# Key sums of an attention block by wide products with ones, and a reordered head, in an attention and bilinear feed-forward kernel

## The chip, the cores and the metric

The kernel runs on one core of a Trainium2 chip. The metric is the device time of one execution in microseconds, the median of several runs. The engines named below are TensorE (PE, matrix products; PEld are its weight loads), VectorE (DVE), ScalarE (ACT), GpSimd (POOL) and SyncE (SP), whose queue issues the DMA transfers here.

## The reference

Two blocks follow each other. Attention has 8 batches, 12 heads, 448 positions and 64 features a head; q and k are normalized by their root mean square and scaled by gains. The result, 3584 tokens of 768 features, goes through a bilinear feed-forward block with 1536 inner features.

```
def rmsnorm(x, g):
    rms = np.sqrt(np.mean(x * x, axis=-1, keepdims=True) + 1e-06)
    return x / rms * g
q_n, k_n = (rmsnorm(q, g_q), rmsnorm(k, g_k))
scores = scale * np.matmul(q_n, k_n.transpose(0, 1, 3, 2))
scores = scores - np.max(scores, axis=-1, keepdims=True)
attn = np.exp(scores)
attn = attn / (np.sum(attn, axis=-1, keepdims=True) + 1e-09)
x = np.matmul(attn, v)            # then (B,H,S,D) -> (B*S, H*D)
out = (x @ w_a) * (x @ w_b) @ w_out
```

The attention inputs are float32. The three weight matrices are float64 and reach the kernel as pairs of 32-bit words.

## The kernel before, in words

**The work.** Attention goes by pairs of heads: 6 pairs a batch, 48 in all. The 448 positions are split into four chunks of 112 (NJ = 4). For pair p, `loads` brings k, q and v; `normalize` squares and reduces k and q (L289 or L291, L297), takes the mean (L306), raises it to the power -0.5 on GpSimd (L310) and scales q with it (L314); `transposes` turns both (L331) and copies them out of PSUM with the gain (L336, L341 or L343). `scores` makes, chunk by chunk of keys, the transposed scores of both heads (L357) and their exponentials (L363, with k's scale folded in), which land as ET, keys on partitions. `values` multiplies ET with v and sums over the chunks in PSUM (L376). `sums_over_keys` makes the softmax denominators, `put_out` copies the values into xT (L479) and multiplies them by the inverted sums (L484).

**Key sums.** The first 12 pairs (LEAD = 12) and the others do it in two ways. From pair 12 on, VectorE and GpSimd add the four chunks of ET (L388, L390), two products with a matrix of ones spread the sums over 64 partitions a head (L406, `spread`), and VectorE inverts 128 x 448 values in PSUM (L409, `invert`). For the lead pairs TensorE does it from ET itself: `by_query` uses a 112 x 112 piece of ET as the stationary operand and one column of ones as the moving one, 2 heads x 4 query groups x 4 chunks, 32 products that the trace shows as 64 records (L416); `invert_few` inverts 112 x 8 values (L422), `to_features` spreads them by 8 products (16 records) with the identity (L428).

**The weights.** 72 units of 128 x 384 numbers (`weights`, L213 to L255): 48 of w_a and w_b, four column groups of 12, then 24 of w_out. Each is loaded as raw word pairs and made into float32 by one pass on ScalarE (L241), four on VectorE (L242, L243, L245, L247), a scaling of the low word, and a final add on GpSimd (L255). The low word is scaled by VectorE for every third unit (L250) and by ScalarE and GpSimd for the others (L253, L254). Units of w_a and w_b are staged in the place of w_out, so a w_out unit can only be written after the staging unit that lay there is done; w_out itself is staged in a ring of two buffers ("stage").

**Feed-forward.** `ffn` works by blocks of 384 or 512 tokens: 24 groups of input products (L510) into two PSUM buffers, taken out by ScalarE (L519) and VectorE (L521) into hT, then the output products (L534), which read w_out. There is one hT, and two xT buffers, so block 2 of xT (pairs from 12 on) opens when block 0 has been read.

**The order.** `Plan` writes the order of every engine's instructions before the kernel runs. Each step is booked by `op(engine, us, key, ...)` with a cost, a key and the buffers it reads and writes. The planner lets each engine take the step that can start first; among those that can start within 0.05 us of each other (0.2 us on TensorE) the lowest key goes first, and steps of one `chain` follow each other. Pair p's steps have key p, a weight unit n has n/4 + 1, loads two less, feed-forward products 10000 and more: they fill what is left. On the chip each engine goes through its list in that order.

Of the kernel before, what the change touches and what calls it, by code (L numbers as in the profile page):

```python
# [25 lines left out]
class Plan:  # L26
# [95 lines left out]
def kernel(  # L122
# [36 lines left out]
    NP = B * HP  # L159
# [4 lines left out]
    const = ctx.enter_context(tc.tile_pool(name="const", bufs=1))  # L164
# [9 lines left out]
    def setup(wk):  # L174
        grow = wk.tile([1, 2, D], FP32, tag="sq", name="grow")
        make_identity(nc, ident)
        nc.gpsimd.memset(expo, -0.5)
        nc.gpsimd.memset(ones, 1.0)
        for n, g in enumerate((g_q, g_k)):
            for e in range(2):  # L180
                nc.sync.dma_start(gain[e * D:(e + 1) * D, n:n + 1], g.rearrange("(d o) -> d o", o=1))
            nc.sync.dma_start(grow[:, n], g.rearrange("(o d) -> o d", o=1))

        nc.vector.scalar_tensor_tensor(gain[:, 0:1], gain[:, 0:1], float(D) ** -0.5, gain[:, 1:2],
                                       ALU.mult, ALU.mult)
        nc.vector.tensor_tensor(grow[:, 0], grow[:, 0], grow[:, 1], ALU.mult)
        nc.vector.tensor_reduce(grow[:, 1, 0:1], grow[:, 0], AX, ALU.max, apply_absolute_value=True)
        nc.vector.tensor_scalar(small, grow[:, 1, 0:1], LIMIT * D ** -0.5, None, ALU.is_le)
# [18 lines left out]
    def fast_body(ld, wk, ps_s, ps_o, ps_mm):  # L207
        plan = Plan()
        op, slot = plan.op, plan.slot
        LEAD = 12  # L210


        def weights(n):  # L213

            src, dst, kc, c = units[n]  # L220
            key = n / 4 + 1.0
            w = dst[:, kc, c * WC:(c + 1) * WC]
            wb, hold = w.bitcast(U32), {}
# [13 lines left out]

            lof = lambda: hold["lo"].bitcast(FP32)
            hif = lambda: hold["hi"].bitcast(FP32)
            op("SP", 0.1, key - 2.0, load, writes=[st], kb=384)  # L240
            op("ACT", 0.55, key, lambda: nc.scalar.activation(w, hif(), AF.Abs), [st], [name])  # L241
            op("DVE", 0.4, key, lambda: nc.vector.tensor_scalar(w, w, BELOW, ABOVE, ALU.max, ALU.min), [], [name])  # L242
            op("DVE", 0.4, key, lambda: nc.vector.tensor_scalar(  # L243
                wb, wb, 3, 0x3FFFFFFF, ALU.logical_shift_left, ALU.bitwise_and), [], [name])
            op("DVE", 0.56, key, lambda: nc.vector.scalar_tensor_tensor(  # L245
                wb, hold["hi"], 0xC0000000, wb, ALU.bitwise_and, ALU.bitwise_or), [st], [name])
            op("DVE", 0.56, key, lambda: nc.vector.tensor_scalar(  # L247
                hold["hi"], wb, 0xFF800000, None, ALU.bitwise_and), [name], [st])
            if n % 3 == 0:
                op("DVE", 0.56, key, lambda: nc.vector.scalar_tensor_tensor(  # L250
                    lof(), hold["lo"], 2.0 ** -52, hif(), ALU.mult, ALU.mult), [], [st])
            else:
                op("ACT", 0.55, key, lambda: nc.scalar.activation(lof(), hold["lo"], AF.Copy, scale=2.0 ** -52), [], [st])  # L253
                op("POOL", 1.05, key, lambda: nc.gpsimd.tensor_tensor(lof(), lof(), hif(), ALU.mult), [], [st])  # L254
            op("POOL", 1.05, key, lambda: nc.gpsimd.tensor_tensor(w, w, lof(), ALU.add), [st], [name])  # L255


# [3 lines left out]
        def loads(p, nm):  # L261
# [4 lines left out]
            def emit():  # L266
# [5 lines left out]
                    x = ld.tile([SP, 2, NJ * D], FP32, tag=nm, name=nm + "_sb")  # L272
                    nc.sync.dma_start(x, src[b, h0:h0 + 2].rearrange("h (p j) d -> p h (j d)", j=NJ))
                xs[nm, p] = x
            op("SP", 0.15, p - 2.0, emit, writes=[names[nm, p]], kb=230)

        def normalize(p):

            ms = names["ms", p] = slot("ms", 3)
            for s, nm in enumerate("kq"):  # L280
                sq, x = slot("sq", 1), names[nm, p]

                def square(nm=nm):
# [12 lines left out]
                        rs[p] = wk.tile([SP, 2, 2 * NJ], FP32, tag="ms", name="ms", bufs=3)  # L296
                    nc.vector.tensor_reduce(rs[p][:, "qk".index(nm)], xs["sq", nm, p], AX, ALU.add)  # L297
                if p < LEAD:
                    op("ACT", 0.65, p, square, [x], [sq])
                else:  # L300
                    op("POOL", 1.05, p, square, [x], [sq])
                op("DVE", 0.69, p, reduce, [sq], [ms])

            def mean():
                msf = rs[p].rearrange("p s n -> p (s n)")
# [6 lines left out]
            def apply():  # L312
# [3 lines left out]
                    xs["q", p].rearrange("p h (j d) -> p h j d", d=D),  # L316
                    rs[p][:, 0].rearrange("p (h j) -> p h j ()", j=NJ).to_broadcast([SP, 2, NJ, D]),
                    ALU.mult)
            op("DVE", 0.18, p, mean, [], [ms])
            op("POOL", 2.95, p, root, [], [ms])  # L320
            op("DVE", 0.7, p, apply, [ms, names["q", p]], [slot("qn", 1)])

        def transposes(p):
            sc = slot("sc", 2)
# [17 lines left out]
                else:  # L342
                    nc.vector.tensor_scalar_mul(qkTs[p][:, 0], x, gain[:, 0:1])  # L343
            T = names["qkT", p]
            op("PE", 0.9, p, turn, [names["k", p], "qn#0"], [sc], mode="full")
            op("ACT", 0.55, p, take_k, [sc], [T])
            op("ACT" if p < LEAD else "DVE", 0.68, p, take_q, [sc], [T])

# [45 lines left out]
            else:  # L394
                op("POOL", 2.1, p, emit, [E], [names["sum", p]])

        def sums_over_keys(p, chains):

            su = names["su", p] = slot("su", 1)

            def spread():
                sus[p] = ps_o.tile([P, S], FP32, tag="su", name="su")
                for e in range(2):
                    nc.tensor.matmul(sus[p][e * D:(e + 1) * D, :], lhsT=ones, rhs=sums[p][0:SP, e], start=True, stop=True)  # L406

            def invert():
                nc.vector.reciprocal(sus[p], sus[p])  # L409

            def by_query():
                sus[p] = ps_o.tile([P, S], FP32, tag="su", name="su")
                for e in range(2):
                    for j in range(NJ):
                        for c in range(NJ):
                            nc.tensor.matmul(sus[p][0:SP, e * NJ + j:e * NJ + j + 1],  # L416
                                             lhsT=ETs[p, c][:, e, j * SP:(j + 1) * SP], rhs=ones[:, 0:1],
                                             start=(c == 0), stop=(c == NJ - 1))

            def invert_few():  # L420
                rs["inv", p] = wk.tile([SP, 2 * NJ], FP32, tag="inv", name="inv", bufs=2)
                nc.vector.reciprocal(rs["inv", p], sus[p][0:SP, 0:2 * NJ])  # L422

            def to_features():
                for e in range(2):
                    for j in range(NJ):
                        n = e * NJ + j
                        nc.tensor.matmul(sus[p][e * D:(e + 1) * D, j * SP:(j + 1) * SP],  # L428
                                         lhsT=rs["inv", p][:, n:n + 1].to_broadcast([SP, D]),
                                         rhs=ident[0:SP, 0:SP], start=True, stop=True)  # L430
# [131 lines left out]
            weights(n)  # L562
        for p in range(NP + 1):
            if p < NP:
                for nm in "kqv":
                    loads(p, nm)
                normalize(p)
                transposes(p)
            if p > 0:
                values(p - 1, 2, f"A{p}")  # L570
                values(p - 1, 3, f"A{p}")
                if p - 1 < LEAD:
                    sums_over_keys(p - 1, (f"A{p}", f"B{p}"))
            if p < NP:
                scores(p, 0, f"A{p}")
                scores(p, 1, f"A{p}")
            if p > 0:
                if p - 1 >= LEAD:
                    sums_over_keys(p - 1, (f"A{p}", f"B{p}"))
                put_out(p - 1)  # L580
            if p < NP:
                values(p, 0, f"B{p}")
# [10 lines left out]
                ffn(p // HP - 2)  # L593
        ffn(B - 1)
        with tc.manual_schedule():
            setup(wk)
            plan.run()
        return plan

# [113 lines left out]
```

## Time and profile before

| what | value |
|---|---|
| median of 3 runs | 1896.07 us (1894.4 to 1897.51) |
| profiled execution | 1896.1 us |
| its span, first to last instruction | 1894.2 us |
| mean granted TensorE clock | 0.965 |
| busy: PE, DVE, ACT, POOL | 1853.9, 577.0, 406.2, 488.6 us |
| moved by DMA | 73.55 MB, mean 39 GB/s |

A row of a group has the line, the engine, the operation, the tiles written and read, their shapes and the count, then the busy time in us, the mean of one in ns, and the engine's idle time just before, with what ended it. A row of the timeline has the start and the length in us first. The matmuls' ends are modelled, so two groups can overlap a little.

### The profile page before, as it was taken

Reading aid. Unit: us, or ns where it says so; the run is one execution under the profiler, and the core shown is the slowest. Engines: PE = TensorE matmul, PEld = TensorE weight load, DVE = VectorE, ACT = ScalarE, POOL = GpSimd, SP = SyncE. Lnnn points to the kernel's source line nnn. Section 1 sums busy time; section 2 is a strip of 40 time slices with the busy share of each in tenths; the row PEclk is TensorE's granted clock in tenths of the full one; section 3 lists DMA queues with packets and bytes.
Section 4 is the critical chain, followed back from the end, with each engine's and each line's share of the span. In section 5 each row is a group of like instructions: output and inputs, shape, how many; then the busy total and the mean of one; then the engine's idle time right before and its main releaser. Section 6 shows DMA issues by size and latency. Waiting matters only on the chain.

```text
span 1894.2 us, 16866 instructions
## 1 busy us (share of the span) xinstructions
PE 1853.9 (98%) x6672; PEld 972.7 (51%) x6672; DVE 577.0 (30%) x824; ACT 406.2 (21%) x785; POOL 488.6 (26%) x324
## 2 busy tenths in 40 slices
PE   6799999999999999999999999999999999999998
PEld 3566665544444445544444445554444545554454
DVE  6788445344201441034201442034201430000000
ACT  5455334123201221023200231023201220000000
POOL 4566335234300441034300441034300410000000
PEclk9677889999999999999999999999999999999999
DMA  7451222111000210011100210011100100000000
GB/s 234 135 144 52 71 80 78 44 42 47 25 0 1 60 46 15 0 42 42 30 0 0 56 48 19 1 42 42 30 0 0 42 18 5 1 25 0 0 9 27
DMA packets 87325, 73.55 MB, mean 39 GB/s; under 512 B 49348, under 2 KB 78020, under 8 KB 87236
## 3 DMA queue, kind: packets, MB, share of 16 engines
q1 hardware_dynamic: 87236, 72.38, 13.4%
q8 instruction: 54, 0.88, 0.2%
q14 instruction: 35, 0.29, 0.0%
HBM read 61.34 MB, written 11.01 MB: 38 GB/s over the span
## 4 chain that ended last, share of the span: by engine, by line
PE 97%; DVE 1%; SPq 0%; ACT 0%; POOL 0%; DMA 0%; issue 0%; POOLq 0%; DVEq 0%; ACTq 0%
PE pf L510 46%; PE po L534 23%; PE sc L357 9%; PE o L376 8%; PE su L416 5%; PE pt L331 2%; PE su L406 2%; PE su L428 1%; ACT ET L363 0%; DMA w_out_sb<-in_moe_w_a_dram 0%; POOL sum L390 0%; POOL ms L310 0%; DVE su L409 0%; DVE w_a_sb L245 0%; DVE w_out_sb L247 0%
## 5 line engine op out<-in xcount | busy, mean ns | idle before, releaser
L510 PE MATMUL pf<-xT,w_b_sb 128*128 128x512 f32 (+1 forms) x1152 | 453.7, 542 | 0.0
L510 PE MATMUL pf<-xT,w_a_sb 128*128 128x512 f32 (+1 forms) x1152 | 453.1, 541 | 0.0
L534 PE MATMUL po<-w_out_sb,hT 128*128 128x384 f32 x1344 | 453.1, 490 | 0.0
L534 PEld LDWEIGHTS po<-w_out_sb,hT 128*128 128x128 f32 x1344 | 249.1, 190 | 192.5 <-issue 35.9
L510 PEld LDWEIGHTS pf<-xT,w_b_sb 128*128 128x128 f32 x1152 | 218.4, 191 | 219.4 <-issue 147.2
L510 PEld LDWEIGHTS pf<-xT,w_a_sb 128*128 128x128 f32 x1152 | 216.9, 190 | 217.8 <-issue 144.6
L363 ACT ACTIVATE ET<-sc,ms 112x448 f32<-112x448 f32 x384 | 213.6, 635 | 319.8 <-PE sc L357 317.6
L521 DVE TENSOR_TENSOR hT<-hT,pf 128x384 f32<-128x384 f32 (+1 forms) x96 | 59.6, 621 | 716.7 <-PE pf L510 716.7
L390 POOL TENSOR_TENSOR sum<-sum,ET 112x896 f32<-112x896 f32 x72 | 152.6, 2119 | 442.7 <-DVE sum L388 303.2
L519 ACT COPY hT<-pf 128x384 f32<-128x384 f32 (+1 forms) x96 | 51.1, 533 | 689.4 <-PE pf L510 689.4
L357 PE MATMUL sc<-qkT 64*112 64x448 f32 x768 | 189.0, 615 | 1.2 <-ACT qkT L341 1.2
L376 PE MATMUL o<-ET,v_sb 112*64 112x448 f32 x768 | 171.9, 556 | 0.0
L310 POOL TENSOR_TENSOR ms<-ms,expo 112x16 f32<-112x16 f32 x48 | 141.0, 2938 | 83.0 <-DVE ms L306 82.8
L409 DVE RECIPROCAL su<-su 128x448 f32<-128x448 f32 x36 | 106.8, 2967 | 122.2 <-PE su L406 122.2
L357 PEld LDWEIGHTS sc<-qkT 64*112 64x112 f32 x768 | 66.6, 188 | 103.9 <-issue 93.8
L416 PEld LDWEIGHTS su<-ones,ET 112*112 112x112 f32 x768 | 103.7, 229 | 9.1 <-PE o L376 3.5
L297 DVE TENSOR_REDUCE ms<-sq 112x8 f32<-112x512 f32 x96 | 65.4, 681 | 132.2 <-POOL sq L291 121.7
L416 PE MATMUL su<-ones,ET 112*112 112x1 f32 x768 | 104.7, 273 | 0.0
L376 PEld LDWEIGHTS o<-ET,v_sb 112*64 112x64 f32 x768 | 55.0, 140 | 87.6 <-issue 83.5
L314 DVE TENSOR_TENSOR qn<-q_sb,ms 112x512 f32<-112x512 f32 x48 | 62.9, 1310 | 85.0 <-issue 65.3
L462 POOL COPY xT<-tail 128x384 f32<-128x384 f32 x4 | 2.1, 520 | 311.9 <-PE pf L510 311.9
L543 DVE COPY o_sb<-po 128x384 f32<-128x384 f32 x28 | 15.6, 558 | 143.9 <-PE po L534 143.9
(60 smaller groups left out, 821.1 us busy)
## 6 DMA issues: line engine op xcount, KB each, us to landing
k_sb<-in_k_dram SPq DMA_DIRECT2D x96, 112.0 KB, 2.8
q_sb<-in_q_dram SPq DMA_DIRECT2D x48, 224.0 KB, 2.8
v_sb<-in_v_dram SPq DMA_DIRECT2D x48, 224.0 KB, 2.6
w_out_sb<-in_moe_w_a_dram SPq DMA_DIRECT2D x24, 384.0 KB, 3.9
w_out_sb<-in_moe_w_b_dram SPq DMA_DIRECT2D x24, 384.0 KB, 4.1
raw<-in_moe_w_out_dram SPq DMA_DIRECT2D x24, 384.0 KB, 3.1
out_dram<-o_sb SPq DMA_DIRECT2D x16, 168.0 KB, 2.1
out_dram<-o_sb SPq DMA_DIRECT2D x16, 144.0 KB, 2.0
```

The costliest lines, as they stand in the source:

```text
L297: nc.vector.tensor_reduce(rs[p][:, "qk".index(nm)], xs["sq", nm, p], AX, ALU.add)
L310: nc.gpsimd.tensor_tensor(msf, msf, expo, ALU.pow)
L314: nc.vector.tensor_tensor(qns[p].rearrange("p j h d -> p h j d"), xs["q", p].rearrange("p h (j d) -> p h j d", d=D), rs[p][:, 0].rearrange ...
L357: nc.tensor.matmul(t[:, e, 0:S], lhsT=qkTs[p][rows, 1, c * SP:(c + 1) * SP], rhs=qkTs[p][rows, 0, :], start=True, stop=True)
L363: nc.scalar.activation(E[:, e], scs[p, c][:, e, 0:S], AF.Exp, scale=rs[p][:, 1, 2 * c + e:2 * c + e + 1])
L376: nc.tensor.matmul(os_[p][e * D:(e + 1) * D, :], lhsT=xs["v", p][:, e, c * D:(c + 1) * D], rhs=ETs[p, c][:, e], start=(c == 0), stop=(c == ...
L390: nc.gpsimd.tensor_tensor(sums[p][0:SP], sums[p][0:SP], ETs[p, c], ALU.add)
L409: nc.vector.reciprocal(sus[p], sus[p])
L416: nc.tensor.matmul(sus[p][0:SP, e * NJ + j:e * NJ + j + 1], lhsT=ETs[p, c][:, e, j * SP:(j + 1) * SP], rhs=ones[:, 0:1], start=(c == 0), s ...
L510: nc.tensor.matmul(pfs[m, n][:, 0:N], lhsT=w_sb[:, c, m * P:(m + 1) * P], rhs=xTs[b][:, c, 0:N], start=(c == 0), stop=(c == KA - 1))
L521: nc.vector.tensor_tensor(x, x, y, ALU.mult)
L534: nc.tensor.matmul(held["po"][:, 0:HALF], lhsT=hTs[0][:, m, t * P:(t + 1) * P], rhs=w_out_sb[:, m, h * HALF:(h + 1) * HALF], start=(m == 0 ...
```

## The change

Five things change.

1. For the 12 lead pairs the key sums are made by `spread` too, fed by the four chunks of ET instead of their sum: 4 chunks x 2 heads products with the matrix of ones, summed in PSUM, then `invert` on VectorE. `by_query`, `invert_few` and `to_features` go.
2. The low word of every unit is scaled on VectorE.
3. Normalization (squares, reductions, mean, root, scaling of q) gets key p - 1.5 instead of p, and squares q before k.
4. The units of w_out get keys 11 to 12.9 instead of 13 to 18.75.
5. At the start, the loads of the gains go behind the q, k and v of pair 0, their use becomes a planned step, the test on the gains gets key 20, q is loaded ahead of k, an exponential of 128 zeros is computed first on ScalarE, and the planner books more time for loads on SP.

```
-            key = n / 4 + 1.0
+            key = n / 4 + 1.0 if n < 48 else 11.0 + (n - 48) / 12
...
-            op("SP", 0.1, key - 2.0, load, writes=[st], kb=384)
+            op("SP", 0.4, key - 2.0, load, writes=[st], kb=384)
...
-            if n % 3 == 0:
-                op("DVE", 0.56, key, lambda: nc.vector.scalar_tensor_tensor(
-                    lof(), hold["lo"], 2.0 ** -52, hif(), ALU.mult, ALU.mult), [], [st])
-            else:
-                op("ACT", 0.55, key, lambda: nc.scalar.activation(lof(), hold["lo"], AF.Copy, scale=2.0 ** -52), [], [st])
-                op("POOL", 1.05, key, lambda: nc.gpsimd.tensor_tensor(lof(), lof(), hif(), ALU.mult), [], [st])
+            op("DVE", 0.6, key, lambda: nc.vector.scalar_tensor_tensor(
+                lof(), hold["lo"], 2.0 ** -52, hif(), ALU.mult, ALU.mult), [], [st])
...
-            op("SP", 0.15, p - 2.0, emit, writes=[names[nm, p]], kb=230)
+            op("SP", 0.5 if nm != "k" else 1.0, p - (1.8 if nm == "v" else 2.0), emit, writes=[names[nm, p]], kb=230)
...
-            for s, nm in enumerate("kq"):
+            for s, nm in enumerate("qk"):
...
-                    op("ACT", 0.65, p, square, [x], [sq])
+                    op("ACT", 0.65, p - 1.5, square, [x], [sq])
...
-            op("DVE", 0.18, p, mean, [], [ms])
-            op("POOL", 2.95, p, root, [], [ms])
-            op("DVE", 0.7, p, apply, [ms, names["q", p]], [slot("qn", 1)])
+            op("DVE", 0.18, p - 1.5, mean, [], [ms])
+            op("POOL", 2.95, p - 1.5, root, [], [ms])
+            op("DVE", 0.7, p - 1.5, apply, [ms, names["q", p]], [slot("qn", 1)])
...
-            op("PE", 0.9, p, turn, [names["k", p], "qn#0"], [sc], mode="full")
+            op("PE", 0.9, p, turn, [names["k", p], "qn#0", "gain"], [sc], mode="full")
...
-                for e in range(2):
-                    nc.tensor.matmul(sus[p][e * D:(e + 1) * D, :], lhsT=ones, rhs=sums[p][0:SP, e], start=True, stop=True)
+                xss = [ETs[p, c] for c in range(NJ)] if p < LEAD else [sums[p][0:SP]]
+                for n, x in enumerate(xss):
+                    for e in range(2):
+                        nc.tensor.matmul(sus[p][e * D:(e + 1) * D, :], lhsT=ones, rhs=x[:, e],
+                                         start=(n == 0), stop=(n == len(xss) - 1))
...
-            if p < LEAD:
-                inv = slot("inv", 2)
-                op("PE", 3.2, p, by_query, [names["ET", p, c] for c in range(NJ)], [su], mode="full", chain=chains[0])
-                op("DVE", 0.2, p - 1, invert_few, [su], [inv])
-                op("PE", 0.9, p, to_features, [inv], [su], mode="cols", chain=chains[1])
-            else:
-                op("PE", 0.76, p, spread, [names["sum", p]], [su], mode="cols", chain=chains[1])
-                op("DVE", 3.0, p, invert, [], [su])
+            op("PE", 3.0 if p < LEAD else 0.76, p, spread,
+               [names["ET", p, c] for c in range(NJ)] if p < LEAD else [names["sum", p]],
+               [su], mode="cols", chain=chain)
+            op("DVE", 3.0, p, invert, [], [su])
...
+            if p == 0:
+                op("SP", 3.0, -1.9, load_gains, [], ["gain"], kb=1)
+                op("DVE", 0.2, -1.0, use_gains, [], ["gain"])
+                op("DVE", 0.6, 20.0, judge_gains, ["gain"], [])
...
-                    sums_over_keys(p - 1, (f"A{p}", f"B{p}"))
+                    sums_over_keys(p - 1, f"A{p}")
```

In the chains, a lead pair's sums now stand whole in chain A of the next pair, behind the last two values products and ahead of the first two scores; before, `by_query` stood there and `to_features` at the head of chain B.

More of the change, by code (lines that the diff above doesn't have):

```diff
@@ L172, with setup @@
     w_out_sb = const.tile([P, KO, DM], FP32, name="w_out_sb")
-    def setup(wk):
-        grow = wk.tile([1, 2, D], FP32, tag="sq", name="grow")
+    grow = const.tile([1, 2, D], FP32, name="grow")
+    def setup():
+        nc.scalar.activation(grow, nc.const_aps.tensor(0.0, [1, 2, D], FP32), AF.Exp)
         make_identity(nc, ident)
@@ L178, in setup, with load_gains @@
         nc.gpsimd.memset(ones, 1.0)
+    def load_gains():
         for n, g in enumerate((g_q, g_k)):
@@ L182, in setup, with use_gains, judge_gains @@
             nc.sync.dma_start(grow[:, n], g.rearrange("(o d) -> o d", o=1))
+    def use_gains():
         nc.vector.scalar_tensor_tensor(gain[:, 0:1], gain[:, 0:1], float(D) ** -0.5, gain[:, 1:2],
                                        ALU.mult, ALU.mult)
+    def judge_gains():
         nc.vector.tensor_tensor(grow[:, 0], grow[:, 0], grow[:, 1], ALU.mult)
@@ L298, in normalize @@
                 if p < LEAD:
-                    op("ACT", 0.65, p, square, [x], [sq])
+                    op("ACT", 0.65, p - 1.5, square, [x], [sq])
                 else:
-                    op("POOL", 1.05, p, square, [x], [sq])
-                op("DVE", 0.69, p, reduce, [sq], [ms])
+                    op("POOL", 1.05, p - 1.5, square, [x], [sq])
+                op("DVE", 0.69, p - 1.5, reduce, [sq], [ms])
             def mean():
@@ L395, in add_up, with sums_over_keys @@
                 op("POOL", 2.1, p, emit, [E], [names["sum", p]])
-        def sums_over_keys(p, chains):
+        def sums_over_keys(p, chain):
             su = names["su", p] = slot("su", 1)
@@ L408, in invert @@
             def invert():
                 nc.vector.reciprocal(sus[p], sus[p])
[L411 to L430, printed above, removed]
@@ L564, in fast_body @@
             if p < NP:
-                for nm in "kqv":
+                for nm in "qkv":
                     loads(p, nm)
+            if p == 0:
+                op("SP", 3.0, -1.9, load_gains, [], ["gain"], kb=1)
+                op("DVE", 0.2, -1.0, use_gains, [], ["gain"])
+                op("DVE", 0.6, 20.0, judge_gains, ["gain"], [])
+            if p < NP:
                 normalize(p)
@@ L578, in fast_body @@
                 if p - 1 >= LEAD:
-                    sums_over_keys(p - 1, (f"A{p}", f"B{p}"))
+                    sums_over_keys(p - 1, f"B{p}")
                 put_out(p - 1)
@@ L595, in fast_body @@
         with tc.manual_schedule():
-            setup(wk)
+            setup()
             plan.run()
```

## The prediction

> **What bounds the kernel now.** I read the page first, then the busy times by stretch, the chain of work that ended last, and the groups of instructions of the head.
>
> ```profile
> PE 1853.9 (98%) x6672; PEld 972.7 (51%) x6672; DVE 577.0 (30%) x824; ACT 406.2 (21%) x785; POOL 488.6 (26%) x324
> DVE  6788445344201441034201442034201430000000
> ```
>
> TensorE is occupied for 98% of the span and VectorE for 30%, but the second line shows that VectorE's work sits at the start: 6 to 8 tenths in the first four slices, nought to five later. The change touches the twelve lead pairs and the weight preparation, so only the head counts. I cut the span where the chain shows the sixth pair put out and feed-forward work starting (165.38), and where the last lead pair is through (325.48).
>
> ```profile
> 0.00:165.38 165.38, 132.65 (x746) 92.00 (x746) 126.47 (x235) 84.21 (x170) 91.30 (x85) 0.75 0.53 157
> 165.38:325.48 160.10, 160.10 (x874) 103.31 (x873) 79.49 (x149) 61.50 (x118) 70.70 (x55) 0.85 0.24 67
> 325.48:1894.20 1568.72, 1561.10 (x5056) 777.35 (x5056) 371.08 (x442) 260.54 (x498) 326.59 (x185) 1.00 0.08 23
> ```
>
> The columns are the stretch, its length, then busy time of PE, weight loads, VectorE, ScalarE and GpSimd, the granted clock, and the DMA share. From 325.48 on TensorE runs at clock 1.00 and stops only at the end: those 1568.7 us I keep as they are. The head is different. TensorE idles 165.4 - 132.7 = 32.7 us in the first stretch and none in the second, yet its granted clock is 0.75 and 0.85. One pair of the second stretch, from the chain (start, length, what), shows why:
>
> ```profile
> 173.58 8.79 PE su L416 x64
> 182.37 3.26 PE sc L357 x8
> 185.63 3.02 PE pf L510 x6
> 188.65 1.06 PE su L428 x13
> ...
> 191.50 1.69 PE sc L357 x8
> 193.19 2.13 PE pf L510 x6
> 195.33 0.77 PE pt L331 x8
> 196.10 1.95 PE pf L510 x6
> 198.05 1.65 PE o L376 x8
> ```
>
> The 64 narrow products of the key sums (L416, one moving column each) hold TensorE for 8.79 us, where the planner books 3.2. What follows pays too: eight score products take 3.26 us, and 1.69 a little later; six feed-forward products 3.02, and 1.95 to 2.13 later. So the narrow form costs its own time and a halved clock behind it.
>
> **The change part by part.** The sum is made against the profiled execution: span 1894.2, whole time 1896.1, so 1.9 us lie around the span; the median of the runs shown is 1896.07, the same.
>
> ```profile
> L416 PE MATMUL su<-ones,ET 112*112 112x1 f32 x768 | 104.7, 273 | 0.0
> L357 PE MATMUL sc<-qkT 64*112 64x448 f32 x216 | 67.5, 760 | 1.2 <-ACT qkT L341 1.2
> L376 PE MATMUL o<-ET,v_sb 112*64 112x448 f32 x208 | 53.0, 585 | 0.0
> L510 PE MATMUL pf<-xT,w_b_sb 128*128 128x384 f32 x60 | 23.8, 536 | 0.0
> L510 PE MATMUL pf<-xT,w_a_sb 128*128 128x384 f32 x61 | 22.6, 504 | 0.0
> L428 PE MATMUL su<-ident,inv 112*64 112x112 f32 x192 | 22.5, 320 | 0.0
> L331 PE MATMUL pt<-ident,qn 112*128 112x112 f32 x56 | 8.6, 280 | 20.1 <-DVE qn L314 20.1
> ```
>
> These are TensorE's groups from 0 to 325.48 (busy us, mean ns, idle before). *Removed:* L416 and L428, 104.7 + 22.5 = 127.2 us. *Added:* per lead pair four chunks for two heads, 16 records, with the shape of the values product L376 (112 rows, 64 stationary columns, 448 moving). Eight of those took 1.65 us, so 3.30 us a pair and 39.6 for twelve. They stand behind values in the same tile mode, so no switch is added.
>
> *Head work at full clock after the change.* A lead pair needs 2 x 1.65 (values) + 2 x 1.69 (scores) + 0.77 (transposes) + 3.30 = 10.75 us; twelve need 129.0. The head also holds 27 groups of eight score products, 26 of values and 14 pairs of transposes, that is 3, 2 and 2 beyond the lead: 5.1 + 3.3 + 1.5 = 9.9. It holds 121 feed-forward records, 20 groups of six at 2.04 (mean of 2.13 and 1.95): 40.8. Sum 179.7. Of the present 325.5, the same work without the wide sums is 140.1, removed products 127.2, idle 32.7; the remaining 25.5 is slow clock. So the span after is 1568.7 + 179.7 + L = 1748.4 + L, where L is what TensorE loses in the head by idling or a slow clock, and L is decided by VectorE, which gets all that the other engines give up.
>
> ```profile
> L245 DVE SCALAR_TENSOR_TENSOR w_a_sb<-w_out_sb,w_a_sb 128x384 uint32<-128x384 uint32 x11 | 11.7, 1064 | 0.4
> L243 DVE TENSOR_SCALAR w_a_sb<-w_a_sb 128x384 uint32<-128x384 uint32 x12 | 9.8, 818 | 0.3
> L245 DVE SCALAR_TENSOR_TENSOR w_b_sb<-w_out_sb,w_b_sb 128x384 uint32<-128x384 uint32 x11 | 8.9, 811 | 0.4
> L243 DVE TENSOR_SCALAR w_b_sb<-w_b_sb 128x384 uint32<-128x384 uint32 x11 | 8.3, 757 | 0.3
> L297 DVE TENSOR_REDUCE ms<-sq 112x8 f32<-112x512 f32 x8 | 5.3, 666 | 0.0
> L242 DVE TENSOR_SCALAR w_a_sb<-w_a_sb 128x384 f32<-128x384 f32 x12 | 4.6, 382 | 0.0
> L250 DVE SCALAR_TENSOR_TENSOR w_out_sb<-w_out_sb 128x384 f32<-128x384 uint32 x8 | 4.5, 557 | 0.2
> L247 DVE TENSOR_SCALAR w_out_sb<-w_a_sb 128x384 uint32<-128x384 uint32 x11 | 4.0, 361 | 0.4
> ...
> L314 DVE TENSOR_TENSOR qn<-q_sb,ms 112x512 f32<-112x512 f32 x3 | 3.4, 1121 | 0.0
> L484 DVE TENSOR_TENSOR xT<-xT,su 128x384 f32<-128x384 f32 x4 | 2.2, 554 | 7.7 <-PE su L428 7.7
> ```
>
> These are VectorE's groups from 80 to 160. A unit costs 0.38 (L242) + 0.79 (L243, both matrices) + 0.94 (L245) + 0.36 (L247), and 0.56 more where VectorE scales the low word (L250): 3.0 us. L243 and L247 do passes of one kind and size, 0.79 against 0.36; L245 and L250 likewise, 0.94 against 0.56. The excess of 0.81 a unit is waiting:
>
> ```profile
> 127.94 1.07 POOL L255 TENSOR_TENSOR w_a_sb<-w_a_sb,w_out_sb 128x384 f32<-128x384 f32 x1 [1.48 <-DVE w_out_sb L250]
> 128.17 1.06 DVE L243 TENSOR_SCALAR w_b_sb<-w_b_sb 128x384 uint32<-128x384 uint32 x1
> ```
>
> While GpSimd's add runs to 129.01, a pass of 0.36 takes 1.06 and ends behind it. Per three units GpSimd now has five such passes (three L255, two L254); after the change it has three. I scale the excess, 0.81 x 3/5 = 0.49, and take 2.7 us a unit. The bounds are 2.2 (no excess) and 3.0 (all of it). The Trainium skill (SBUF — State Buffer, Who interferes with whom) says that a VectorE pass in its two-port mode, or with two SBUF inputs, and a GpSimd pass exclude each other for the whole instruction. The trace agrees (1.06 for 0.36). By that rule the moved pass can now be held up in every unit, since it has two SBUF inputs; at one such loss of 0.70 a unit it would be 2.9, and the sum 11 us later.
>
> The second new burden is the reciprocal in PSUM, known from the later pairs:
>
> ```profile
> L409 DVE RECIPROCAL su<-su 128x448 f32<-128x448 f32 x36 | 106.8, 2967 | 122.2 <-PE su L406 122.2
> ```
>
> A lead pair then costs VectorE two reductions 1.33, mean 0.18 (as the planner books it), scaling of q 0.9 (between 0.69 booked and 1.12), division 0.65, reciprocal 2.97: 6.0 us. GpSimd and ScalarE, 91 and 84 busy of the first 165 us, lose work and bound nothing.
>
> *The order.* Normalization of a pair now has key p - 1.5, ahead of the weight units it used to stand behind. This goes:
>
> ```profile
> 59.29 1.01 PE L331 MATMUL pt<-ident,qn 112*128 112x112 f32 x4 [13.08 <-DVE qn L314]
> ```
>
> TensorE's 13.1 us of waiting for the third pair's q is a matter of order, not of capacity. What is late next is VectorE as a whole. The gain loads leave the front of the SP queue:
>
> ```profile
> 4.17 1.32 SPq L270 DMA_DIRECT2D k_sb<-in_k_dram  x2
> 10.23 0.69 DVE L297 TENSOR_REDUCE ms<-sq 112x8 f32<-112x512 f32 x1 [4.03 <-ACT sq L289]
> ```
>
> Six small loads stand ahead of the first k at 4.17. Moved behind pair 0's loads, they let the first reduction start near 7 instead of 10.2. The use of the gains becomes a wait in VectorE's queue with pair 0's and the first units' passes behind it, and the first transposes wait for it: 0 to 2 us, taken at nought, since pair 0's normalization runs beside the landing.
>
> *VectorE's account.* Up to the sixth pair's division it owes 17 units with key up to 5 (46 us), six pairs (36), the next normalization (2.4): from 7 to 91 without a wait, about 105 if a seventh of that time is waiting (now it idles 24% of the first stretch, behind TensorE). TensorE has 6 x 10.75 = 65 us of work until then: 40 lost. Up to the last unit of the third matrix it owes 72 x 2.7 = 194, 12 x 6.0 = 72, twelve hT products 7, two more pairs in part 6: from 7 to 286, with 8% of waiting 309 (a third of the present 24%, since it is now the scarce engine). TensorE's work that needs no third matrix is 129 + 9.9 + all 48 groups of the first block's input products (98), the rest of a pair and two begun output products (10): 247. So L = 309 - 247 = 62, and without waits 40, set by the first part.
>
> Sum: -127.2 + 39.6 - 25.5 + (62 - 32.7) = -83.8. Span 1810, time **1812**.
>
> **The rivals.**
>
> *VectorE keeps up.* The excess nearly vanishes and waits are few; L is then 30 to 40: 1780 to 1790, say 1786. For it: the 24% that VectorE idles now is time in which TensorE was the slow one. Against it: 48 more passes and 12 reciprocals, about 62 us, on an engine busy 126 of 165.
>
> *The third matrix comes late.*
>
> ```profile
> L255 POOL TENSOR_TENSOR w_out_sb<-w_out_sb,raw x24: 1004/1011/1472, 195.2 to 360.1; 128x384 f32<-128x384 f32 x24
> ```
>
> Its 24 units go through a ring of two buffers, load, ScalarE, VectorE, GpSimd, each load waiting for the add two units before. Now they take (360.1 - 195.2)/23 = 7.2 us each, but nothing hurries them: in the chain the first output product follows 54 us of input products. After the change they can start near 205 (unit 36 done). At 4.5 us they end at 309, as VectorE's account has it; at 5.8 at 338, L = 91 and the time is 1841.
>
> *The same, slower than before.* The ring decides alone from 147 us of L on, an end at 394, which is 8.2 us a unit. At 9 us: end 412, L = 165, time 1915. It needs a worse pace than the unhurried 7.2, with loads that stall in the SP queue behind q, k and v.
>
> *The clock stays low.* TensorE will idle over a third of the first 105 us. After the 13 us gap above, four transposes took 1.01 us, where eight take 0.77. If all of the first six pairs ran at half clock they would need 129 us, end near 137, and 32 us are added: 1844. Against it: pairs overlap, so most gaps are short. The Trainium skill (TensorE: Matmul & The Clock Gate, What's actually happening) has the clock fall to half after one idle window of about 3.4 us. The trace shows this behind gaps, but also behind L416 with no gap at all (3.26 against 1.69), so narrow products seem to count as idling.
>
> *The change doesn't deliver,* since the written order hangs together by something else: near 1896.
>
> ```profile
> 325.48 54.38 PE pf L510 x168
> 379.85 3.87 PE po L534 x12
> ```
>
> Against it: nothing but TensorE's own work stands in the second stretch, and these two rows show that the first output products had waited for input products alone.
>
> **How the numbers follow.** My forecast has 0.55 (1812); VectorE keeping up 0.16 (1786); third matrix late 0.18 (1841); clock low 0.06 (1844); slower 0.03 (1915); no change 0.02. The range of 1782 to 1846 covers units at 2.3 to 3.0 us and third-matrix ends from 280 to 341; it leaves out the low end of the second case and the last two. About 0.2% is what a measurement of this kernel tells from no change (three runs spread over 3.1 us). Faster 0.95, same 0.02, slower 0.03.
>
> **What would show it.** Right: sums of 16 wide products of 3.3 us; scores behind them at 1.69; granted clock above 0.9 in the second stretch; 48 reciprocals; VectorE over 85% busy to about 300; first output product between 290 and 330. Wrong: VectorE with long idle while TensorE waits (order), the first output product after 340 (ring), or a loss beyond the head.

## The result and the profile after

The changed kernel takes 1820.18 us (median of four runs, 1819.57 to 1821.77) against 1895.63 for the kernel before (1894.4 to 1897.51): a ratio of 0.960, 95% interval 0.9586 to 0.9619. The profiled execution spans 1817.8 us at a mean granted clock of 0.991. Of the experiments further down, one execution of run 2 took 4860 us beside three of about 1887, and the ratio of run 2 is that of the three.

First the page of the changed kernel: busy times, then the slices of VectorE and of the granted clock.

```profile
PE 1761.7 (97%) x5904; PEld 860.4 (47%) x5904; DVE 640.5 (35%) x872; ACT 384.3 (21%) x738; POOL 457.3 (25%) x276
...
DVE  7999998640023410443004420245002420000000
...
PEclk8999999999999999999999999999999999999999
```

TensorE has lost 92 us of busy time and 768 instructions. VectorE is now in its highest tenth for five slices of 45 us, and TensorE's clock is low in the first slice alone. The same by stretch (length, then busy time of PE, weight loads, VectorE, ScalarE, GpSimd, then clock, DMA share, GB/s):

```profile
0.00:120.00 120.00, 86.30 (x369) 33.12 (x370) 104.26 (x178) 67.78 (x134) 52.41 (x41) 0.90 0.58 174
120.00:200.00 80.00, 79.92 (x350) 35.50 (x351) 77.20 (x118) 40.68 (x79) 37.66 (x26) 1.00 0.37 102
200.00:340.00 140.00, 124.26 (x450) 62.58 (x450) 123.55 (x196) 38.40 (x77) 74.23 (x50) 0.98 0.31 87
340.00:1817.80 1477.80, 1471.23 (x4740) 729.22 (x4736) 335.45 (x383) 237.49 (x451) 292.98 (x160) 1.00 0.08 22
```

TensorE idles 33.7 us up to 120 and 15.7 us between 200 and 340, 49.5 in the head; before it idled 32.7, all in the first stretch. What it does there, and what it waits for (busy us, mean ns, idle before; up to 340 us):

```profile
L362 PE MATMUL sc<-qkT 64*112 64x448 f32 x250 | 58.3, 586 | 4.9 <-DVE qkT L348 3.6 <-ACT qkT L346 1.3
L491 PE MATMUL pf<-xT,w_b_sb 128*128 128x384 f32 x144 | 52.2, 508 | 9.8 <-DVE hT L502 9.8
...
L411 PE MATMUL su<-ET,ones 112*64 112x448 f32 x192 | 39.9, 559 | 0.0
L515 PE MATMUL po<-w_out_sb,hT 128*128 128x384 f32 x48 | 16.4, 492 | 0.0
L336 PE MATMUL pt<-ident,qn 112*128 112x112 f32 x64 | 10.1, 287 | 15.2 <-DVE qn L319 15.2
L336 PE MATMUL pt<-ident,k_sb 112*128 112x112 f32 x64 | 10.0, 282 | 13.7 <-ACT ET L368 8.8 <-DMA k_sb<-in_k_dram 4.9
```

The wide sums (L411) take 39.9 us in place of 127.2. A score record costs 58.3/250 = 0.233 us instead of 67.5/216 = 0.313, since no narrow products stand before it (run 2 shows this). VectorE's groups up to 350 us:

```profile
L415 DVE RECIPROCAL su<-su 128x448 f32<-128x448 f32 x15 | 44.4, 2958 | 2.0 <-PE su L411 2.0
L258 DVE SCALAR_TENSOR_TENSOR w_out_sb<-w_out_sb 128x384 f32<-128x384 uint32 x48 | 29.6, 617 | 1.3
L252 DVE TENSOR_SCALAR w_a_sb<-w_a_sb 128x384 uint32<-128x384 uint32 x24 | 26.3, 1096 | 0.8
...
L319 DVE TENSOR_TENSOR qn<-q_sb,ms 112x512 f32<-112x512 f32 x18 | 18.0, 1002 | 7.8 <-POOL ms L315 7.4 <-PE pt L336 0.3
L254 DVE SCALAR_TENSOR_TENSOR w_out_sb<-raw,w_out_sb 128x384 uint32<-128x384 uint32 x24 | 18.0, 750 | 0.8
L252 DVE TENSOR_SCALAR w_b_sb<-w_b_sb 128x384 uint32<-128x384 uint32 x24 | 17.8, 741 | 0.7
```

The numbers after the bar are the busy time and the mean: L252 took 0.36 at its shortest, and for w_a takes 1.10 in the mean. By line, the five passes of the 72 units take 29.5 (L251), 60.0 (L252), 48.3 (L254), 27.2 (L256) and 45.3 us (L258): 210.3, or 2.92 a unit. Two rows give the ends of the head, the first feed-forward product and the adds of the third matrix (shortest, median and longest in ns, first and last start):

```profile
L491 PE MATMUL pf<-xT,w_a_sb x1152: 486/591/697, 119.8 to 1743.8; 128*128 128x384 f32 x96, 128*128 128x512 f32 x96
...
L260 POOL TENSOR_TENSOR w_out_sb<-w_out_sb,raw x24: 1005/1060/2398, 200.2 to 327.3; 128x384 f32<-128x384 f32 x24
```

Feed-forward work starts at 119.8 (before 167.0), the last add of w_out at 327.3 (before 360.1), and the first output product at 297.1 (before 379.7).

### The profile page after: what moved, and what is told of

Read it like the earlier page. It is cut to its first block, busy times and chain, and to the rows that moved or that the text cites. A ratio compares the mean times of both kernels' runs of the same rounds, so it can differ in the third digit from the quotient of the medians.

```text
span 1817.8 us, 15323 instructions
## 1 busy us (share of the span) xinstructions
PE 1761.7 (97%) x5904; PEld 860.4 (47%) x5904; DVE 640.5 (35%) x872; ACT 384.3 (21%) x738; POOL 457.3 (25%) x276
## 5 line engine op out<-in xcount | busy, mean ns | idle before, releaser
L415 DVE RECIPROCAL su<-su 128x448 f32<-128x448 f32 x48 | 142.3, 2964 | 147.3 <-PE su L411 147.3
L362 PE MATMUL sc<-qkT 64*112 64x448 f32 x768 | 172.2, 568 | 4.9 <-DVE qkT L348 3.6
L315 POOL TENSOR_TENSOR ms<-ms,expo 112x16 f32<-112x16 f32 x48 | 141.8, 2953 | 26.7 <-DVE ms L311 25.1
L362 PEld LDWEIGHTS sc<-qkT 64*112 64x112 f32 x768 | 61.7, 174 | 111.6 <-issue 93.5
L524 DVE COPY o_sb<-po 128x384 f32<-128x384 f32 x28 | 15.6, 557 | 144.6 <-PE po L515 144.6
L296 POOL TENSOR_TENSOR sq<-k_sb 112x512 f32<-112x512 f32 x36 | 38.0, 1056 | 71.5 <-DMA k_sb<-in_k_dram 70.2
L460 ACT COPY xT<-o 128x384 f32<-128x384 f32 (+1 forms) x48 | 24.2, 505 | 145.8 <-PE o L381 123.9
```

What stands on the lines that cost most here:

```text
L315: nc.gpsimd.tensor_tensor(msf, msf, expo, ALU.pow)
L362: nc.tensor.matmul(t[:, e, 0:S], lhsT=qkTs[p][rows, 1, c * SP:(c + 1) * SP], rhs=qkTs[p][rows, 0, :], start=True, stop=True)
```

## The experiments

The theory after the result: TensorE is no longer the bound in the head; VectorE's backlog of weight units and pairs is. Its rival: the written order of the steps costs the time, whatever VectorE's load. The expectations call the theory V and a rival O; K, in 7, 10 and 11, is the theory that the early keys of the third matrix cost time. All runs stand here together; "idle" is what TensorE idles in the first 380 us, then come the start of the first feed-forward product and that of the last add of the third matrix. The kernel before, run again beside each, took 1895.6 to 1897.2 us in the median. The fifth part of the change, the start, was not taken back by itself.

| kernel | us | 95% of the ratio to before | idle | first ff | last add |
|---|---|---|---|---|---|
| changed | 1820.18 | 0.9586 to 0.9619 | 49.5 | 119.8 | 327.3 |
| 1 wide sums alone | 1838.62 | 0.9673 to 0.9706 | 65.2 | 137.7 | 362.4 |
| 2 all but the wide sums | 1886.99 | 0.9924 to 0.9963 | 20.1 | 154.9 | 348.9 |
| 3 low words as before | 1832.44 | 0.9643 to 0.9675 | 58.7 | 126.8 | 328.9 |
| 4 one pass more | 1846.09 | 0.9712 to 0.9745 | 72.3 | 113.0 | 354.0 |
| 5 GpSimd's add left out | 1786.31 | 0.9404 to 0.9436 | 25.3 | 105.4 | (none) |
| 6 normalization at key p | 1826.68 | 0.9607 to 0.9641 | 52.8 | 124.1 | 326.8 |
| 7 third matrix later | 1849.26 | 0.9731 to 0.9764 | 73.2 | 121.2 | 378.7 |
| 8 measured costs | 1830.51 | 0.9632 to 0.9665 | 57.5 | 111.0 | 336.5 |
| 9 add on VectorE | 1834.17 | 0.9651 to 0.9683 | 62.2 | 108.0 | 319.8 |
| 10 = 9, third matrix later | 1836.88 | 0.9667 to 0.9699 | 64.3 | 107.5 | 365.8 |
| 11 = 8, third matrix later | 1845.42 | 0.9712 to 0.9744 | 70.8 | 110.0 | 386.6 |
| 12 sums of squares on ScalarE | 1826.32 | 0.9613 to 0.9645 | 56.0 | 125.3 | 304.6 |

**1. The wide sums alone.** The kernel before, with the changed function for the key sums and nothing else.

```
-                op("PE", 3.2, p, by_query, ...)
-                op("DVE", 0.2, p - 1, invert_few, [su], [inv])
-                op("PE", 0.9, p, to_features, ...)
+            op("PE", 3.0 if p < LEAD else 0.76, p, spread, ...)
+            op("DVE", 3.0, p, invert, [], [su])
```

> The kernel before with the wide key sums alone: low words, keys and the start as before. Theory V (the sums give TensorE's time back, and what is left in the head is VectorE's backlog): most of the gain comes from this part, 1795 to 1830 us, with TensorE's sums at 3.2 us a pair and scores behind them at 1.7 us. Rival O (the new order and the moved low words carry the gain, the wide sums only shift the bound to VectorE): above 1860.

58.5 us of the 75.5 come from the wide sums alone. That is most of the gain, but the time lies 9 us above the range that the theory gave. The price in the old order is one wait (us in all, times, longest):

```profile
PE pt L331 <- DVE qn L314: 33.3, 5, 18.3
```

**2. The reverse:** the changed kernel with the narrow sums of before.

> The changed kernel with the narrow sums of before: all other parts of the change kept. V: TensorE is the bound again, 1870 to 1900 us, with sums of about 8.5 us a pair and scores behind them at 3.3 us. O: the order and the low words carry a good part, below 1860.

The other four parts are worth 10 us without the wide sums, and 18 with them (1 against the changed kernel). The stretches show why: from 120 us on TensorE is nearly always busy, but its clock stays low, with no gap that could explain it (same columns as above):

```profile
0.00:120.00 120.00, 100.43 (x560) 68.62 (x561) 84.02 (x170) 56.17 (x112) 47.95 (x40) 0.77 0.56 168
120.00:200.00 80.00, 79.49 (x436) 54.49 (x436) 59.24 (x115) 33.09 (x64) 32.05 (x24) 0.77 0.33 95
200.00:280.00 80.00, 80.00 (x448) 51.72 (x448) 55.65 (x106) 25.00 (x48) 31.29 (x25) 0.85 0.26 76
```

One pair of this run shows which of the narrow sums' two kinds of product it is. The eight score products right behind L421 (one moving column) take 3.33 us; those behind L433 (112 moving columns) take 1.76 again:

```profile
161.38 8.76 PE L421 MATMUL su<-ones,ET 112*112 112x1 f32 x64
170.07 3.33 PE L362 MATMUL sc<-qkT 64*112 64x448 f32 x8
...
176.46 1.13 PE L433 MATMUL su<-ident,inv 112*64 112x112 f32 x13
...
179.32 1.76 PE L362 MATMUL sc<-qkT 64*112 64x448 f32 x8
```

**3. Low words as before,** two of three on ScalarE and GpSimd, in the changed kernel.

```
-            op("DVE", 0.6, key, ... lof(), hold["lo"], 2.0 ** -52, hif() ...)
+            if n % 3 == 0: op("DVE", 0.56, key, ...)
+            else: op("ACT", 0.55, key, ...); op("POOL", 1.05, key, ...)
```

> The changed kernel with the low words scaled as before (VectorE for one unit in three, ScalarE and GpSimd for the rest). VectorE saves 48 passes of 0.63 us, 30 us. V with the exclusion of GpSimd's and VectorE's passes: each of the 48 passes given to GpSimd holds VectorE up by about what it saves (0.5 to 0.7 us), 1812 to 1826. V by capacity alone, without that exclusion: near 1795. O: 1820, nothing moves.

A miss: 12 us slower. VectorE's unit passes did fall, but only from 210.3 to 192.5 us: 29.4 us of scaling went, and 11.6 came back as longer passes beside a GpSimd that is busy 71.5 of the first 120 us instead of 52.4. Yet less load made it slower. By 120 us 26 units are done instead of 23, and the pairs are later:

```profile
PE pt L340 <- DVE qn L323: 19.9, 3, 14.4
PE sc L366 <- DVE qkT L352: 14.7, 3, 6.9
```

For the third pair it isn't GpSimd's load that delays them: GpSimd's root ends at 42.6 us here and at 42.2 in the changed kernel, but VectorE scales q at 46.1 instead of 42.2, behind passes of weight units that the planner put first.

**4. One VectorE pass more a unit,** the clamp (L251) done twice, which leaves the numbers as they are.

> The changed kernel with VectorE's first pass of every weight unit (the clamp) done twice, which changes no value: 72 passes of about 0.4 us, 29 us more on VectorE and nothing on any other engine. V: most of it shows, 1836 to 1852. O (VectorE's load is hidden behind waits of another kind): 1816 to 1826.

All unit passes now sum to 231.9 us, 21.6 more (the 72 passes would be some 29 by L251; the second clamp now meets GpSimd's add, and L252's old pass falls from 60.0 us to 30.2), and the time grows by 25.9. The third matrix ends 26.7 us later. Added work on VectorE shows in full, and a little more.

**5. GpSimd's add left out,** so the weights lack the bits of the low words.

```
-            op("POOL", 1.05, key, lambda: nc.gpsimd.tensor_tensor(w, w, lof(), ALU.add), [st], [name])
```

> The changed kernel without GpSimd's add of the scaled low word to each weight unit, so the weights lack their last bits. VectorE does every pass that it did. If GpSimd's adds hold VectorE's passes up (0.65 us a unit, 47 us in 72 units, from the mean durations against their shortest), VectorE's unit falls from 2.92 to about 2.3 us and the time to 1775 to 1800. If the longer passes have another cause: 1815 to 1823.

VectorE's work is the same in kind and count, but its passes are near their shortest (groups up to 360 us):

```profile
L258 DVE SCALAR_TENSOR_TENSOR w_out_sb<-w_out_sb 128x384 f32<-128x384 uint32 x48 | 27.6, 576 | 1.4
...
L252 DVE TENSOR_SCALAR w_b_sb<-w_b_sb 128x384 uint32<-128x384 uint32 x24 | 10.8, 448 | 0.6
...
L252 DVE TENSOR_SCALAR w_a_sb<-w_a_sb 128x384 uint32<-128x384 uint32 x24 | 10.4, 433 | 0.8
```

The unit falls from 2.92 to 2.37 us, 39.3 us over 72 units, and the time by 33.9. So VectorE lost some 39 us in passes held up while GpSimd added. The run also takes an add of about 1 us out of every unit's way, so how much of the 33.9 us comes from VectorE's passes alone isn't shown.

**9. The add on VectorE,** which gives the right weights without GpSimd.

```
-            op("POOL", 1.05, key, lambda: nc.gpsimd.tensor_tensor(w, w, lof(), ALU.add), [st], [name])
+            op("DVE", 0.58, key, lambda: nc.vector.tensor_tensor(w, w, lof(), ALU.add), [st], [name])
```

> The changed kernel with the same add done by VectorE instead of GpSimd: VectorE gets 72 passes of about 0.56 us, 40 us, and loses whatever GpSimd's adds cost it. With the exclusion of the two engines' passes (47 us) the two cancel: 1805 to 1822, although VectorE does all five passes and the add. Without it VectorE's 40 us show: 1845 to 1860.

It falls between the two: 14 us slower than the changed kernel. The passes are short again (L252 of w_a has a mean of 359 ns, the add 0.56 us) and feed-forward work starts at 108.0 instead of 119.8; up to 200 TensorE is 9.6 us ahead. Then it stands still (the chip's order on TensorE: start, length, what, idle before):

```profile
239.54 2.05 PE L411 MATMUL su<-ET,ones 112*64 112x448 f32 x10
260.80 3.30 PE L362 MATMUL sc<-qkT 64*112 64x448 f32 x8 [19.21 <-DVE qkT L348]
...
282.89 1.65 PE L491 MATMUL pf<-xT,w_a_sb 128*128 128x384 f32 x2 [11.06 <-DVE w_a_sb L260]
```

In that time VectorE makes mostly units of the third matrix, whose keys (11 and more) come before those of pair 12 and of the last units of w_a and w_b (up to 12.75).

**8. The planner told the measured costs.**

```
-  0.4, 0.4, 0.56, 0.56, 0.6 for L251, L252, L254, L256, L258
+  0.42, 0.83, 0.67, 0.38, 0.63
```

> The changed kernel, only the planner's costs of VectorE's five passes set to the means that the profile after shows (0.42, 0.83, 0.67, 0.38, 0.63 instead of 0.4, 0.4, 0.56, 0.56, 0.6 us): same instructions, another order. By 120 us VectorE had done 23 units where the sixth pair's key needs 17. If the planner's too low costs let units run ahead of the pairs: the first feed-forward product comes before 115 instead of 120 us, and 1803 to 1815. If only VectorE's total work counts: 1817 to 1824.

A miss: 10 us slower. The first feed-forward product comes at 111.0, as hoped, but TensorE then waits 14.7 us for one unit of w_a, and the third matrix ends 9 us later.

**7, 10 and 11. The third matrix later,** in the changed kernel and on top of 9 and 8.

```
-            key = n / 4 + 1.0 if n < 48 else 11.0 + (n - 48) / 12
+            key = n / 4 + 1.0 if n < 48 else 13.0 + (n - 48) / 12
```

> The changed kernel, only the units of w_out at keys 13 to 14.9. Here the waits at 200 to 280 us were short (10 us for hT, 4 us for q), since the planner's low costs let units of w_a and w_b run ahead. K: small, 1810 to 1822. Rival (w_out at the head of the order is what the changed kernel needs, its last unit ends at 327 us and the output products wait for it): 1828 or more.

> The changed kernel with the add on VectorE and the units of w_out at keys 13 to 14.9 instead of 11 to 12.9. With the add on VectorE alone the first feed-forward product came at 108 us (120 in the changed kernel), but at 241 to 261 and 272 to 283 us TensorE waited for pair 12's q and for the last units of w_a while VectorE worked on w_out units with lower keys. Theory K (the early keys of w_out cost about 30 us there): 1800 to 1812 us and those two waits gone. Rival (VectorE's total work decides, the waits only move behind the w_out units): 1826 or more.

> The changed kernel with the planner's true costs and the units of w_out at keys 13 to 14.9. True costs alone brought the first feed-forward product to 111 us and then 15 and 9 us of TensorE's waiting at 240 to 280. K: 1802 to 1815. Rival (total work): 1824 or more.

The key that was meant to clear the wait of 9 made all three slower than their own base, by 29 us on the changed kernel and 15 on 8; of 10 and 9, which are 3 us apart, the intervals overlap. In 10 TensorE no longer waits for units of w_a, but it waits 35.8 us for VectorE's copies of q (L348), where 9 had 19.2: the waits moved. In 7, the last 100 us of the head and its main wait read:

```profile
280.00:380.00 100.00, 71.17 (x275) 32.03 (x275) 82.44 (x115) 31.29 (x64) 51.53 (x35) 0.85 0.29 83
```

```profile
PE sc L362 <- DVE qkT L348: 37.3, 6, 9.4
```

The third matrix is done at 379 instead of 327, by 380 us TensorE has had 24 output products to fill with instead of 120, and pairs 12 to 17 wait for VectorE's copies. So the early key of the third matrix is worth 29 us in the changed kernel.

**6. Normalization back at key p.**

```
-                op("DVE", 0.69, p - 1.5, reduce, [sq], [ms])
+                op("DVE", 0.69, p, reduce, [sq], [ms])
```

and likewise in its five other steps.

> The changed kernel with normalization at key p again. The prediction gave the new key 13 us of TensorE's waiting for the third pair's q; but the changed kernel still waits 10.4 us there, and the first output product comes late by VectorE's backlog anyway. Theory V: 1819 to 1830. If the new key is worth its 13 us: 1832 or more.

6.5 us slower, and TensorE's waits for scaled q are 27.3 us in eight pieces instead of 15.2 in three.

**12. A version meant to be better:** ScalarE sums the squares of the lead pairs while it makes them.

```
-                        nc.scalar.activation(t, flat, AF.Square)
+                        for g in range(2 * NJ):
+                            nc.scalar.activation(t[:, g], flat[:, g], AF.Square,
+                                                 accum_out=rs[p][:, "qk".index(nm), g:g + 1])
```

> The changed kernel, but for the twelve lead pairs ScalarE sums the squares itself while it makes them (16 short squares a pair, one to each group of 64, with their sum), so VectorE loses two reductions of 0.68 us a pair, 24 in all, 16 us. Theory (VectorE's backlog in the head sets the time): most of the 16 us shows, 1803 to 1812. Rival (the pairs are paced by ScalarE and by waits for single results, not by VectorE's load): ScalarE gets some 2 us a pair more ahead of each pair's exponentials, so nothing is gained or the time grows: 1820 or more.

The rival holds: 6 us slower. ScalarE's price was not 2 us a pair more but 5.8 (groups up to 330 us):

```profile
L297 ACT ACTIVATE sq<-k_sb 112x64 f32<-112x64 f32 x96 | 23.2, 249 | 6.6 <-DMA k_sb<-in_k_dram 6.5
...
L297 ACT ACTIVATION_READ_ACCUMULATOR sq<-k_sb 112x1 f32 x96 | 18.6, 194 | 0.0
```

16 x (0.25 + 0.19) = 7.1 us a pair, against 1.3 for two long squares. VectorE did get ahead, the third matrix ends 22.7 us earlier than in the changed kernel, but the pairs are late:

```profile
PE pt L341 <- DVE qn L324: 19.6, 3, 13.2
PE o L386 <- ACT ET L373: 11.2, 7, 4.2
```

In the changed kernel these are 15.2 and 3.9 us. By 200 us TensorE has been busy 153.0 us instead of 166.2.

**What follows.** Both theories are partly right. VectorE's time is on the path: 21.6 us more of it costs 25.9 (4), 39.3 less gains 33.9 (5). But in 3 and 12 VectorE had less to do, and in 9 as much, and each was slower than the changed kernel: its time is worth something only where it reaches the step that TensorE waits for. The planner chooses anew for each set of costs and keys, so no run holds the order fixed and varies the load alone, and how much of TensorE's remaining 49.5 us another order would save stays open. Of five changes of keys, costs or engines that were to win time (8 to 12), none did; only 5, which isn't the whole computation, beats the changed kernel.

## Why the prediction was right

Forecast 1812, range 1782 to 1846; measured 1820, span 1817.8 against 1810. The likeliest case happened: VectorE was busy 273.9 of the first 300 us, and the first output product came at 297.1. The mechanism held, but that the time came within 8 us is in part luck, since two terms of L were off by some 17 us each and in opposite directions.

- **Removed and added.** 16 wide products a lead pair: 39.6 forecast, 39.9 measured. With the narrow products gone the clock came back, from 0.75 and 0.85 to 0.90 up to 120 us and 0.98 to 1.00 after. Run 2 shows the narrow sums to be the cause: all else changed, they keep the clock at 0.77. The prediction weighed the page of the Trainium skill that has the clock fall after an idle window (TensorE: Matmul & The Clock Gate, What's actually happening): run 2 has the low clock without such a window too.
- **The rest of the span.** 1748.4 + L was the form; so L, what TensorE loses in the head, is 1817.8 - 1748.4 = 69.4 against 62. Idling makes 49.5 of it; the other 19.9 are slow clock and whatever the estimate of 179.7 us of work at full clock is off; no run splits them.
- **The mis-sized term: VectorE's unit.** The prediction scaled the excess by GpSimd's passes and took 2.7 us; it is 2.92. 72 x 0.22 = 16 us, which is most of the 18 us by which the last unit came late (last pass at 326.7, forecast 309). The step that failed was the scaling: three fifths of GpSimd's passes left 0.70 us of hold-ups a unit (2.92 less the 2.22 of the prediction's terms without any). The 0.81 that was scaled had been read from 80 to 160 us; over all 72 units of the kernel before, the same sum gives 2.85 a unit and 0.63 of hold-ups, so they did not shrink with the passes at all. Run 5 shows where they come from. The rule of the Trainium skill (SBUF — State Buffer, Who interferes with whom), which the prediction gave as 2.9 us a unit, came nearer to the size. But it expected the loss in the moved pass, and that one is hardly held up (L258: a mean of 0.63 against 0.56); the loss lies in L252 (0.83 against 0.36). Nor does it give the better time: by the prediction's own account 0.2 us more a unit is 72 x 0.2 x 1.08 = 15.6 us and not 11, so the forecast by it is 1828.
- **Why 18 us late cost only 7.** L was taken as the last unit's end less 247 us of other work. With 326.7 that gives 80 and a time of 1830; the 69.4 lie 10 below it. The other work was put too low. These are groups of TensorE in the changed kernel from 0 to 327.3, when the last add starts:

```profile
L381 PE MATMUL o<-ET,v_sb 112*64 112x448 f32 x240 | 63.0, 595 | 4.1 <-ACT ET L368 3.9
L362 PE MATMUL sc<-qkT 64*112 64x448 f32 x240 | 54.4, 573 | 2.2 <-ACT qkT L346 1.3 <-DVE qkT L348 0.9
L515 PE MATMUL po<-w_out_sb,hT 128*128 128x384 f32 x36 | 12.2, 489 | 0.0
```

These are 30 groups of eight scores and 30 of values, where the account had 27 and 26, with 16 pairs of transposes for its 14 and 36 output products on the parts of w_out that were ready. At the forecast's own prices TensorE had then done 264 us of work and not 247. Those 17 us take back most of what the late unit cost.
- **The first part.** The sixth pair was to be divided at about 105; it is divided at 116.2, and feed-forward work starts at 119.8. The mis-sized unit explains little of it: 17 units at 0.22 more are 4 us. The account also took it that VectorE makes only the 17 units with key up to 5 by then. It had finished 23, and six more at 2.92 are 18 us: the planner let units run ahead of the pairs. Run 8, with other costs in the planner alone, starts at 111.0, and run 5, with units of 2.37, at 105.4. The 40 us to be lost there came as 33.7 of idling beside a clock of 0.90.
- **The third pair's q, wrong.** The prediction said that this wait of 13.1 us goes with the new key. It is still there, as the order of VectorE and TensorE shows:

```profile
28.56 2.96 DVE L415 RECIPROCAL su<-su 128x448 f32<-128x448 f32 x1
...
34.63 0.68 DVE L302 TENSOR_REDUCE ms<-sq 112x8 f32<-112x512 f32 x1
...
38.03 0.68 DVE L302 TENSOR_REDUCE ms<-sq 112x8 f32<-112x512 f32 x1
...
42.19 1.33 DVE L319 TENSOR_TENSOR qn<-q_sb,ms 112x512 f32<-112x512 f32 x1
...
43.57 1.01 PE L336 MATMUL pt<-ident,qn 112*128 112x112 f32 x4 [10.44 <-DVE qn L319]
```

The key only settles ties: between these rows stand fifteen passes of weight units, and ahead of them all the first pair's reciprocal, an addition of this very change. What was called a matter of order alone looks like one of capacity too; no run splits the two. By run 6 the key is worth 6.5 us.
- **The low words, right by another way.** They were booked as a burden on VectorE. Run 3 shows that putting them back costs 12 us: the burden is real (17.8 us of passes), but the order that the planner makes without it is worse.
- **Not foreseen:** 9.8 us in which the feed-forward products, the filler, wait for VectorE to take out hT.
- **The start.** The gains cost VectorE a wait of 0.9 us (0 to 2 forecast), and its first reduction starts at 4.2, earlier than the 7 forecast.
- **The rivals.** VectorE did not keep up (1786); in run 5, where most hold-ups are gone, the time is 1786 too, but that kernel is not the whole computation and a unit costs it 2.37. The third matrix did not come at its ring's pace: its adds follow each other every (327.3 - 200.2)/23 = 5.5 us, while VectorE is busy 123.6 of 140 us and waits only 3.5 us in all for a unit of that matrix; in run 9 the same ring turned every (319.8 - 206.4)/23 = 4.9 us.

## What to carry to other kernels

When an edit moves the bound to another engine, price that engine's passes with their hold-ups by the neighbours that will still run beside them, not in proportion to how many are taken away; read the hold-ups over all instances and not in one stretch. Give the last-needed data (here w_out) an early enough place that its consumer becomes filler, and expect that freeing the new bound engine helps only if the order lets the freed time reach the step that is waited for. Products with one moving column are dear twice: for their own time and for the clock of what follows.

## What the runs showed of the hardware

- Where products with a single moving column recur, issued without gaps, the mean granted clock is 0.77 while TensorE is busy 79.5 of 80 us (run 2, 120 to 200); with wide products in their place it is 1.00. The products right behind them take about twice their time (3.33 us against 1.76).
- GpSimd's add of 128 x 384 lengthens VectorE's integer pass L252 of w_a from a mean of 359 ns (run 9, no such add) to 1096, but the reciprocal, whose input and output lie in PSUM, kept its 2952 to 2967 ns in all 48 instances, seven of which had such an add beside them.
- A sum in ScalarE's accumulator costs a second instruction: 194 ns to read it, behind a 249 ns square of 112 x 64.
